# Linear attention into a feed-forward block on one core: x of three token tiles by three products with block-diagonal weights, small copies on another engine, weight sums taken earlier

## The chip, the cores and the metric

The kernel runs on one core of a Trainium2 chip. The metric is device time in microseconds (us), the median of several executions, lower is better. Its engines work side by side, each through its own list of instructions in order: TensorE (PE: matrix products, results in PSUM), VectorE (DVE), ScalarE (ACT), GpSimd (POOL) and SyncE (SP), which here issues almost all DMA transfers.

## The reference, cut to what matters

Shapes: 8 batches, 8 heads, 576 positions, head size 64; 4608 tokens, model width 512, inner width 2048, all float32.

```python
q_s = softmax(q, axis=-1)                  # over the 64 features of a head
k_s = softmax(k, axis=2)                   # over the 576 positions
kv  = einsum('bhsd,bhse->bhde', k_s, v)    # 64 x 64 for each batch and head
x   = einsum('bhsd,bhde->bhse', q_s, kv)   # as 4608 x 512, heads side by side
h   = x @ w_in                             # 512 -> 2048
g   = maximum(h, 0) + log1p(exp(-abs(h)))  # softplus
out = g @ w_out                            # 2048 -> 512
```

## The kernel before

**Tiles.** The 4608 tokens are nine tiles (t = 0 to 8) of 512. Heads are taken in pairs (h = 0 to 3), so that two heads of 64 fill 128 partitions. A batch has 576 positions, so each tile lies over two batches. The inner width is 16 blocks of 128 (j = 0 to 15). The words of the change count tiles from one: its tiles 3 to 5 are t = 2, 3 and 4 here.

**Split numbers.** Almost all products run in a fast float32 form that keeps fewer bits. A factor a is split into a high part (rounded by a copy, mostly on ScalarE) and a low part (a minus the high part, mostly on VectorE), and a product is the sum of three: high by high, low by high, high by low.

**Stages.** Tile 0 goes through while the weights arrive and are split; tile 1 uses the split weights where they lie in SBUF. During tile 1 each split weight is also stored to a DRAM copy (`keep_w`, 1 MB a block), because later tiles need its place. Tile 2 fetches the blocks back one by one (`fetch_w`) into five places in turn. Tiles 3 to 8 are three pairs, p = 0 to 2: there the first product (x by w_in) of two tiles and two blocks is done with seven block products in place of eight. This scheme needs sums and differences of weight blocks (`sum_unit`, s = 0 to 7) and of parts of x (`operand_unit`). The weight sums are computed once, stored to DRAM (`kept_sums`) and fetched back for each pair (`fetch_sums`).

**x of a tile.** For a tile and a head pair, `q` is turned by a VectorE transpose into a PSUM bank (`flip`), split, multiplied by the small matrices kv, and taken out again. Two forms exist:
- `x_unit`: kv is block-diagonal, 128 x 128, with the two heads' 64 x 64 matrices on the diagonal, as high and low parts (`kv_hi`, `kv_lo`); three products per batch in the tile. Before the change only tile 1 uses it.
- `x_sided`: for each head of the pair, a 128 x 128 operand stacks that head's high and low parts, so that two products do the work of three. In exchange each copy and subtraction is done for two halves of 64 partitions, and two partial results in two PSUM banks must be brought together (`cross`: two ScalarE copies; `join`: two VectorE additions). Before the change tiles 2 to 8 use it, and from batch 2 on the kv matrices are written in that form (`high_sided`, four ScalarE copies, `low_sided`, two VectorE operations).
`side_kv` converts kv matrices that were written block-diagonal to the sided form, or clears the quarters that the sided form needs empty.

**The order.** Nothing is planned at build time: a string, `ORDER`, lists some 2,100 tokens, and each token emits a few instructions. Every engine does its share of them in just that order, and so does SyncE's DMA queue, so that a transfer that has to wait holds back those listed behind it. The tokens that matter here:
- `Ui`, `Ai`, `Oi` (i = 16 t + j): first product of tile t and block j (12 matmuls of 512 columns), softplus, second product (12 matmuls), for tiles 0 to 2; `H t.j.0`, `H t.j.1`: the split of its result (ScalarE, then VectorE).
- `C p.s.i`: pair p, step s; i = 0 to 6 the seven products (6 matmuls each), 7 to 16 the ScalarE and VectorE work on them. `I t.j.part`: half a second product (6 matmuls).
- `X p.c.name`: operands of a pair from x: `hB11` a high part (ScalarE), `lB11` a low part, `T1` a sum (both VectorE).
- `x t.h.i`: the steps of `x_unit` or `x_sided`. `k b.h.i`: batch b's kv: 0 maximum, 4 subtraction (both VectorE), 5 exponential (ScalarE), 6 product, 7 scale, 8 and 9 high and low part. `n`: load of a coming k and v block (two buffers in turn). `q t.i`: softmax of q: 0, 1, 2 maxima, 3, 4 subtraction, 5, 6 exponential, 7, 8 sums, 9 reciprocal, 10, 11 multiplication. `L t`: load of q.
- `Y s.i`: weight sums s: 0 and 1 put two weight blocks together again, 2 to 5 add, 6 high part, 7 low part, 8 store. `D k`: store of a split weight. `R 0.k`, `R 1.s`, `R 2.n`: fetch of a weight, of two second-product weights, of sums. `F`: a finished output block. `V i.h`: `side_kv`.

In the softmax of q the 64 features of a head lie in two neighbouring groups of 32 partitions. Maxima and sums of the partner group are brought over by four copies of 32 x 64 (`swapped`, line 552, and `swap`, line 588), on VectorE for all tiles but the first.

The weight sums of step s go through a staging place, `STAGE[s]`. Before the change these are the places w5 to w11 and w14, and the units are spread over tile 2, each after the fetch of its two weight blocks.

Of the kernel before, what the change touches and what calls it, by code (L numbers as in the profile page):

```python
# [46 lines left out]
STAGE = ("w5", "w6", "w7", "w8", "w9", "w10", "w11", "w14")  # L47
# [18 lines left out]
    k2.0.7 k2.1.7 k2.0.8 q2.8 U21 D5 G18 A21 q2.5 k2.0.9 U22 D6 q2.7 k2.2.0 O17 O18 k2.2.1 G19 A22 k2.3.0 O19 G20
    O20 G21 k2.1.8 k2.1.9 k2.2.2 k2.2.3 k2.3.1 k2.3.2 O21 G22 O22 k2.2.4 U23 D7 k2.2.5 k2.2.6 n A23 q2.9 U24 D8 V1.2
    U25 D9 k2.2.7 q2.10 q2.11.1 k2.2.8 k2.2.9 k2.3.3 k2.3.4 A24 U26 k2.3.5 R0.0 H1.7.0 V0.3 H1.8.0 H1.7.1 A25 H1.8.1
    x2.0.0 L3 O23 V0.2 x2.0.1 k3.0.0 A26 x2.0.2 D10 O24 H1.9.0 H1.9.1 k3.0.4 R0.1 q3.0 k2.3.6 H1.10.0 U27 n k2.3.7
    H1.10.1 k2.3.8 k2.3.9 q3.1 x2.0.3 A27 O25 D11 x2.0.4 R0.2 U28 x2.1.0 x2.0.5 k3.1.0 x2.1.1 H1.11.0 x2.1.2 D12 O26  # L70
# [1 line left out]
    q3.3 x2.2.1 U30 H1.13.0 x2.2.2 x2.1.5 D15 H1.13.1 x2.1.6 x2.2.3 q3.4 A30 O28 x2.2.4 R0.4 q3.5 U31 x2.3.0 Y0.1
    x2.3.1 Y1.0 q3.6 x2.3.2 O29 x2.2.5 Y0.2 H1.14.0 x2.2.6 A31 H1.14.1 q3.7 x2.3.3 H1.15.0 q3.8 O30 x2.3.4 H1.15.1
    k3.0.6 x2.3.5 x2.3.6 k3.1.6 n k3.0.7 q3.9 k3.0.8 U32 k3.0.9 L4 k3.1.7 q3.10 k3.1.8 U33 q3.11 A32 H2.0.0 k3.1.9 n
    k3.2.0 O31 A33 H2.0.1 Y0.3 k3.2.4 Y1.1 U34 F1.0 q4.0 F1.1 F1.2 Y0.4 Y1.2 F1.3 k3.3.0 H2.1.0 U35 A34 H2.1.1 Y0.5
    k3.3.4 q4.1 k3.2.5 O32 Y1.3 q4.2 k3.3.5 Y1.4 A35 q4.3 k3.2.6 R0.5 k3.3.6 n k3.2.7 Y1.5 k3.2.8 O33 k3.3.7 k3.3.8
    k3.2.9 x3.0.0 k3.3.9 x3.0.1 U36 H2.2.0 x3.0.2 R0.6 H2.3.0 Y0.6 H2.2.1 x3.0.3 H2.3.1 O34 x3.0.7 n Y2.0 A36 x3.0.8
    Y1.6 U37 x3.1.0 H2.4.0 k4.0.0 x3.1.1 R0.7 x3.1.2 O35 A37 H2.4.1 k4.0.4 Y2.1 k4.1.0 x3.1.3 H2.5.0 U38 x3.1.7
    H2.5.1 R0.8 Y2.2 x3.1.8 O36 x3.2.0 A38 k4.1.4 x3.2.1 Y2.3 k4.0.5 x3.2.2 U39 Y3.0 R0.9 k4.1.5 q4.4 H2.6.0 Y3.1
    q4.5 x3.2.3 H2.6.1 O37 x3.2.7 q4.7 q4.6 x3.2.8 A39 U40 x3.3.0 R0.10 q4.8 x3.3.1 Y2.4 H2.7.0 x3.3.2 O38 A40  # L80
    H2.7.1 q4.9 x3.3.3 H2.8.0 Y4.0 U41 x3.3.7 R0.11 H2.8.1 Y2.5 x3.3.8 Y2.6 q4.10 O39 A41 Y4.1 q4.11 k4.0.6 Y3.2
    H2.9.0 Y4.2 R0.12 k4.1.6 k4.0.7 n H2.9.1 k4.0.8 U42 k4.1.7 Y5.0 k4.1.8 k4.0.9 Y5.1 k4.1.9 O40 Y0.7 A42 Y5.2 Y0.8
    Y2.7 U43 Y5.3 H2.10.0 Y3.3 Y5.4 k4.2.0 R0.13 H2.10.1 O41 A43 Y5.5 n k4.2.4 Y5.6 Y1.7 X0.0.hB11 X0.1.hB11 Y5.7
    U44 H2.11.0 Y2.8 H2.11.1 Y3.4 Y4.3 Y3.5 Y4.4 O42 Y3.6 X0.0.lB11 R0.14 k4.3.0 A44 Y4.5 X0.1.lB11 Y4.6 U45 Y5.8
    k4.3.4 Y3.7 k4.2.5 Y4.7 Y1.8 O43 k4.3.5 Y6.0 H2.12.0 Y6.2 A45 H2.12.1 Y6.1 R0.15 k4.2.6 Y6.3 H2.13.0 k4.3.6
    k4.2.7 n Y6.4 k4.2.8 U46 k4.3.7 H2.13.1 k4.3.8 k4.2.9 x4.0.0 k4.3.9 x4.0.1 O44 R2.0 Y6.5 A46 x4.0.2 X0.0.hB21
    X0.1.hB21 X0.0.lB21 Y6.6 R0.0 X0.1.lB21 x4.0.3 n U47 Y7.0 x4.0.7 Y7.1 H2.14.0 x4.0.8 O45 x4.1.0 A47 X0.0.T1
    x4.1.1 Y3.8 H2.14.1 x4.1.2 C0.0.0 H2.15.0 Y6.7 Y4.8 x4.1.3 C0.0.7 H2.15.1 I2.14.0 x4.1.7 Y7.2 Y7.3 I2.14.1
    x4.1.8 R0.1 X0.0.hT1 I2.15.0 x4.2.0 X0.1.T1 x4.2.1 I2.15.1 X0.0.lT1 Y6.8 X0.1.hT1 x4.2.2 F2.0 F2.1 X0.1.lT1
    x4.2.3 Y7.4 x4.2.7 Y7.5 R2.1 F2.2 x4.2.8 F2.3 x4.3.0 X0.0.hB22 R0.2 X0.0.T3 x4.3.1 X0.0.lB22 X0.0.hT3 x4.3.2  # L90
# [5 lines left out]
    k5.1.5 I3.1.1 C0.1.14 C0.1.15 q5.2 C0.2.0 R0.6 q5.3 C0.1.16 I3.2.0 C0.2.7 q5.4 H3.3.0 C0.2.1 H3.3.1 q5.5 C0.2.2
    C0.2.8 q5.7 I3.2.1 C0.2.9 C0.2.3 R0.7 q5.6 C0.2.4 C0.2.10 I3.3.0 H3.4.0 C0.2.11 H3.4.1 C0.2.12 C0.2.5 q5.8
    C0.2.6 C0.2.13 R2.4 C0.2.14 I3.3.1 C0.2.15 q5.9 C0.2.16 C0.3.0 R0.8 H3.5.0 H3.5.1 I3.4.0 C0.3.7 q5.10 q5.11
    C0.3.1 C0.3.2 C0.3.8 q6.0 I3.4.1 C0.3.9 q6.1 C0.3.3 H3.6.0 R0.9 q6.2 C0.3.4 C0.3.10 H3.6.1 I3.5.0 C0.3.11 q6.3
    C0.3.12 C0.3.5 C0.3.6 C0.3.13 R2.5 C0.3.14 I3.5.1 C0.3.15 q6.4 C0.3.16 C0.4.0 R0.10 H3.7.0 H3.7.1 I3.6.0 C0.4.7  # L100
    q6.5 C0.4.1 C0.4.2 q6.6 C0.4.8 q6.7 I3.6.1 C0.4.9 q6.8 C0.4.3 R0.11 H3.8.0 C0.4.4 C0.4.10 H3.8.1 I3.7.0 C0.4.11
    q6.9 C0.4.12 C0.4.5 C0.4.6 C0.4.13 R2.6 C0.4.14 k5.0.6 C0.4.15 q6.10 I3.7.1 C0.4.16 n k5.0.7 q6.11 C0.5.0 k5.0.8
    R0.12 I3.8.0 k5.0.9 C0.5.7 H3.9.0 H3.9.1 C0.5.1 k5.1.6 C0.5.8 k5.2.0 C0.5.2 k5.1.7 I3.8.1 C0.5.9 n k5.1.8 k5.2.4
    C0.5.3 H3.10.0 k5.1.9 C0.5.4 C0.5.10 R0.13 H3.10.1 I3.9.0 C0.5.11 C0.5.12 C0.5.5 k5.3.0 C0.5.6 R2.7 C0.5.13
    I3.9.1 C0.5.14 k5.3.4 C0.5.15 k5.2.5 C0.6.0 R0.14 I3.10.0 k5.3.5 C0.6.7 C0.5.16 k5.2.6 k5.3.6 k5.2.7 n C0.6.1
    k5.3.7 k5.2.8 C0.6.2 k5.3.8 k5.2.9 x5.0.0 I3.10.1 k5.3.9 x5.0.1 C0.6.8 C0.6.9 x5.0.2 C0.6.3 R0.15 H3.11.0 n
    H3.12.0 H3.11.1 x5.0.3 C0.6.10 C0.6.4 x5.0.7 H3.12.1 I3.11.0 x5.0.8 C0.6.5 x5.1.0 C0.6.11 x5.1.1 I3.11.1 R2.8
    C0.6.12 x5.1.2 C0.6.6 C0.6.13 C0.6.14 x5.1.3 R1.0 C0.6.15 C0.7.0 x5.1.7 I3.12.0 x5.1.8 C0.7.7 C0.6.16 X1.0.hB11
    C0.7.1 x5.2.0 k6.0.0 x5.2.1 C0.7.2 H3.13.0 x5.2.2 X1.1.hB11 I3.12.1 C0.7.9 C0.7.8 k6.0.4 x5.2.3 H3.14.0 R1.1
    C0.7.3 H3.13.1 x5.2.7 C0.7.4 x5.2.8 I3.13.0 x5.3.0 X1.0.hB21 k6.1.0 x5.3.1 I3.13.1 x5.3.2 R1.2 C0.7.10 x5.3.3  # L110
    k6.1.4 C0.7.5 x5.3.7 C0.7.11 k6.0.5 x5.3.8 C0.7.6 R2.9 H3.14.1 k6.1.5 C0.7.15 k6.0.6 X1.0.lB11 C0.7.16 I3.14.0 n
    k6.0.7 X1.1.lB11 C0.7.13 I3.14.1 X1.0.lB21 H3.15.0 C0.7.14 H3.15.1 k6.1.6 H4.0.0 R1.3 k6.0.8 I3.15.0 H4.0.1
    k6.1.7 k6.0.9 I3.15.1 F3.0 F3.1 k6.2.0 I4.0.0 F3.2 H4.1.0 F3.3 H4.1.1 n k6.1.8 I4.0.1 k6.2.4 k6.1.9 I4.1.0
    H4.2.0 X1.1.hB21 R1.4 H4.2.1 C0.7.12 I4.1.1 X1.1.lB21 I4.2.0 H4.3.0 k6.3.0 I4.2.1 H4.3.1 H4.4.0 I4.3.0 k6.3.4
    R1.5 H4.4.1 k6.2.5 I4.3.1 I4.4.0 k6.3.5 H4.5.0 k6.2.6 H4.5.1 k6.3.6 k6.2.7 n k6.2.8 I4.4.1 k6.3.7 k6.3.8 k6.2.9
    I4.5.0 x6.0.0 R1.6 k6.3.9 x6.0.1 I4.5.1 H4.6.0 x6.0.2 H4.7.0 H4.6.1 x6.0.3 n H4.7.1 I4.6.0 x6.0.7 x6.0.8 I4.6.1
    R1.7 x6.1.0 I4.7.0 X1.0.T1 x6.1.1 I4.7.1 H4.8.0 x6.1.2 X1.0.hT1 H4.9.0 H4.8.1 x6.1.3 H4.9.1 I4.8.0 x6.1.7
    X1.0.lT1 R0.0 x6.1.8 I4.8.1 x6.2.0 I4.9.0 H4.10.0 x6.2.1 H4.10.1 I4.9.1 x6.2.2 I4.10.0 H4.11.0 H4.11.1 R0.1
    x6.2.3 X1.1.T1 I4.10.1 x6.2.7 I4.11.0 x6.2.8 H4.12.0 X1.1.hT1 I4.11.1 x6.3.0 X1.0.hB22 H4.12.1 x6.3.1 C1.0.0
# [964 lines left out]
```

## Time and profile before

| | |
|---|---|
| median of 3 runs | 861.38 us (859.04 to 862.44) |
| the profiled execution's own time | 863.02 us |
| its span, first to last instruction | 861.2 us |
| TensorE busy | 834.0 us, 97% |
| VectorE busy | 592.4 us, 69% |
| ScalarE busy | 503.0 us, 58% |
| GpSimd busy | 57.4 us, 7% |
| moved by DMA | 197.9 MB |

The times come from one profiled execution. Matmuls overlap: one lasts about 390 ns in the list of groups, while a new one starts every 0.22 us, so that a busy TensorE can still be behind its best pace. Idle time of an engine counts only where it delays the one that sets the end.

### The profile page before, as it was taken

Reading aid. Unit: us, or ns where it says so; the run is one execution under the profiler, and the core shown is the slowest. Engines: PE = TensorE matmul, PEld = TensorE weight load, DVE = VectorE, ACT = ScalarE, POOL = GpSimd, SP = SyncE. Lnnn points to the kernel's source line nnn. Section 1 sums busy time; section 2 is a strip of 40 time slices with the busy share of each in tenths; the row PEclk is TensorE's granted clock in tenths of the full one; section 3 lists DMA queues with packets and bytes.
Section 4 is the critical chain, followed back from the end, with each engine's and each line's share of the span. In section 5 each row is a group of like instructions: output and inputs, shape, how many; then the busy total and the mean of one; then the engine's idle time right before and its main releaser. Section 6 shows DMA issues by size and latency. Waiting matters only on the chain.

```text
span 861.2 us, 11885 instructions
## 1 busy us (share of the span) xinstructions
PE 834.0 (97%) x4332; PEld 678.2 (79%) x4332; DVE 592.4 (69%) x1003; ACT 503.0 (58%) x795; POOL 57.4 (7%) x128
## 2 busy tenths in 40 slices
...
GB/s 339 375 261 153 28 129 251 165 339 398 152 187 171 282 388 397 260 240 196 257 244 231 254 213 231 257 245 196 239 206 255 186 186 205 244 196 164 181 243 49
DMA packets 74522, 197.91 MB, mean 230 GB/s; under 512 B 4832, under 2 KB 37344, under 8 KB 59104
## 3 DMA queue, kind: packets, MB, share of 16 engines
...
q8 instruction: 34, 0.56, 0.3%
...
## 4 chain that ended last, share of the span: by engine, by line
PE 87%; DVE 6%; DMA 3%; ACT 2%; issue 1%; SPq 0%; POOL 0%; ACTq 0%; POOLq 0%; DVEq 0%
PE po L789 13%; PE po L791 13%; PE po L790 13%; PE ph L865 9%; PE ph L867 9%; PE ph L866 9%; PE ph L746 4%; PE ph L747 4%; PE ph L748 4%; PE att L680 2%; PE att L471 2%; DMA w<-in_q 2%; PE ph L1023 1%; DMA kvt<-in_kv 1%; PE po L785 1%
## 5 line engine op out<-in xcount | busy, mean ns | idle before, releaser
L791 PE MATMUL po<-w,g_lo 128*128 128x512 f32 x472 | 184.6, 391 | 2.3 <-DVE g_lo L764 2.3
L789 PE MATMUL po<-w,g_hi 128*128 128x512 f32 x472 | 185.8, 394 | 0.8 <-ACT g_hi L761 0.8
L790 PE MATMUL po<-w,g_hi 128*128 128x512 f32 x472 | 184.3, 390 | 0.0
L791 PEld LDWEIGHTS po<-w,g_lo 128*128 128x128 f32 x472 | 88.9, 188 | 22.4 <-DVE g_lo L764 3.8
L789 PEld LDWEIGHTS po<-w,g_hi 128*128 128x128 f32 x472 | 89.0, 189 | 19.5 <-ACT g_hi L761 1.2
L790 PEld LDWEIGHTS po<-w,g_hi 128*128 128x128 f32 x472 | 88.9, 188 | 17.9
L764 DVE TENSOR_TENSOR g_lo<-g,g_hi 128x512 fp32r<-128x512 f32 x94 | 64.0, 684 | 48.5 <-ACT g_hi L761 48.1
L867 PE MATMUL ph<-w,x 128*128 128x512 f32 x192 | 75.4, 393 | 2.2 <-DVE w L828 2.2
L865 PE MATMUL ph<-w,x 128*128 128x512 f32 x192 | 76.0, 396 | 1.4 <-ACT w L824 1.4
L866 PE MATMUL ph<-w,x 128*128 128x512 f32 x192 | 75.2, 392 | 0.0
L761 ACT CAST g_hi<-g 128x512 fp32r<-128x512 f32 x94 | 57.9, 619 | 26.6 <-PE po L790 24.2
L881 DVE TENSOR_TENSOR g<-ph,g 128x512 f32<-128x512 f32 x48 | 33.1, 690 | 46.3 <-PE ph L867 46.1
L746 PE MATMUL ph<-x,w 128*128 128x512 f32 x160 | 63.5, 397 | 0.0
L902 ACT ACTIVATE w<-w 128x512 f32<-128x512 f32 x36 | 22.8, 632 | 69.0 <-DVE w L881 68.9
L747 PE MATMUL ph<-x,w 128*128 128x512 f32 x160 | 62.4, 390 | 0.0
L748 PE MATMUL ph<-x,w 128*128 128x512 f32 x160 | 62.4, 390 | 0.0
L906 ACT ACTIVATE g<-ph 128x512 f32<-128x512 f32 x24 | 14.4, 598 | 54.2 <-PE ph L867 54.0
L865 PE MATMUL ph<-w,w 128*128 128x512 f32 x114 | 44.8, 393 | 0.0
L755 ACT ACTIVATE g<-ph 128x512 f32<-128x512 f32 x48 | 28.5, 597 | 27.8 <-PE ph L748 24.7
L881 DVE TENSOR_TENSOR w<-ph,g 128x512 f32<-128x512 f32 x36 | 24.9, 691 | 28.9 <-PE ph L867 28.8
L867 PE MATMUL ph<-w,w 128*128 128x512 f32 x114 | 44.6, 391 | 0.0
L866 PE MATMUL ph<-w,w 128*128 128x512 f32 x114 | 44.6, 391 | 0.0
...
## 6 DMA issues: line engine op xcount, KB each, us to landing
w<-kept SPq DMA_DIRECT2D x50, 1024.0 KB, 4.9
x<-sums SPq DMA_DIRECT2D x24, 1024.0 KB, 4.9
...
kept<-w SPq DMA_DIRECT2D x15, 1024.0 KB, 8.9
spare<-kept SPq DMA_DIRECT2D x14, 1024.0 KB, 5.0
...
```

Of the source, the lines that this page charges most:

```text
L746: nc.tensor.matmul(ph, lhsT=w_hi, rhs=x_hi, start=h == 0, stop=False)
L747: nc.tensor.matmul(ph, lhsT=w_lo, rhs=x_hi, start=False, stop=False)
L748: nc.tensor.matmul(ph, lhsT=w_hi, rhs=x_lo, start=False, stop=h == HP - 1)
L761: nc.scalar.copy(soft[t, j][1], g)
L764: nc.vector.tensor_tensor(out=g_lo, in0=g, in1=g_hi.bitcast(F32), op=ALU.subtract)
L789: nc.tensor.matmul(po, lhsT=g_hi[:, ms], rhs=w_hi, start=j == 0, stop=False)
L790: nc.tensor.matmul(po, lhsT=g_hi[:, ms], rhs=w_lo, start=False, stop=False)
L791: nc.tensor.matmul(po, lhsT=g_lo[:, ms], rhs=w_hi, start=False, stop=j == NJ - 1)
L865: nc.tensor.matmul(ph, lhsT=w_hi, rhs=x_hi, start=c == 0 and i in (0, 1, 3, 4), stop=False, **more)
L866: nc.tensor.matmul(ph, lhsT=w_lo, rhs=x_hi, start=False, stop=False, **more)
L867: nc.tensor.matmul(ph, lhsT=w_hi, rhs=x_lo, start=False, stop=c == 1, **more)
L881: nc.vector.tensor_tensor(out=out, in0=b, in1=a, op=ALU.add)
```

## The change

1. `SIDED = 5`: `x_unit` with block-diagonal kv is used for tiles 1 to 4, `x_sided` from tile 5 on. `x_unit` gets a step `take`, with which tiles 3 and 4 copy the result from PSUM to the place of q; tile 2 splits it straight from PSUM. kv of batches 2 to 4 is written by `high` and `low`. `side_kv` now converts batch 4's matrices, in pair 0, ahead of tile 5, and no longer batch 1's ahead of tile 2.
2. `LATE_Q = 3`: from tile 3 on the partner copies of q's softmax run on ScalarE, as steps of their own in the order (`q t.12`, `q t.13`).
3. `STAGE`: the first four sums' staging places are w1, w15, w0 and the spare one, the others w5 to w8. In the new order the units Y0 to Y3 stand in tile 1 and read the split weights that still lie in SBUF, ahead of the fetches for tile 2; Y4 to Y7 stand in tile 2.
4. The order from tile 1's middle to pair 2's beginning is new. The numbers of the tokens are the same but for the `x` and `q` steps named above; as many transfers are listed as before.

```diff
+SIDED = 5
+LATE_Q = 3
-STAGE = ("w5", "w6", "w7", "w8", "w9", "w10", "w11", "w14")
+STAGE = ("w1", "w15", "w0", "spare", "w5", "w6", "w7", "w8")
 ORDER = """
...
-    A28 H1.11.1 k3.1.4 x2.0.6 k3.0.5 D13 q3.2 x2.1.3 U29 Y0.0 x2.1.4 R0.3 k3.1.5 H1.12.0 O27 A29 x2.2.0 H1.12.1 D14
...
-    Y7.6 X0.0.T2 x4.3.3 X0.0.lT3 x4.3.7 X0.0.T4 X0.0.hT2 x4.3.8 X0.0.hT4 R0.3 X0.1.T3 X0.1.hB22 X0.1.lB22 X0.1.hT3
-    X0.1.T2 X0.0.lT2 X0.1.hT2 X0.1.lT2 X0.1.lT3 C0.0.1 X0.1.T4 X0.1.hT4 C0.0.2 C0.0.8 R0.4 X0.0.lT4 C0.0.3 X0.1.lT4
...
+    k2.2.8 k2.2.9 k2.3.3 k2.3.4 A24 U26 k2.3.5 D10 H1.7.0 H1.8.0 H1.7.1 A25 H1.8.1 Y0.0 D11 k2.3.6 x2.0.0 A26 O23 n
+    Y0.1 x2.0.1 k2.3.7 Y1.0 k2.3.8 x2.0.2 Y1.1 x2.0.3 H1.9.0 k2.3.9 O24 Y3.0 x2.0.4 D12 H1.9.1 Y3.1 Y3.2 x2.1.0 U27
+    D13 H1.10.0 Y3.3 x2.0.5 x2.1.1 H1.10.1 Y3.4 x2.1.2 D14 O25 Y3.5 A27 x2.2.0 Y3.6 Y1.2 Y0.2 Y3.7 D15 x2.1.3
+    H1.11.0 Y1.3 U28 Y0.3 x2.2.1 H1.11.1 x2.1.4 x2.2.2 x2.1.5 Y3.8 Y1.4 x2.3.0 x2.2.3 A28 Y1.5 O26 x2.3.1 Y2.0 Y1.6
+    Y0.4 L4 x2.3.2 Y2.1 Y1.7 x2.3.3 H1.12.0 L3 U29 Y0.5 H1.12.1 Y0.6 Y2.2 k3.0.0 R0.0 Y0.7 O27 A29 Y2.3 k3.0.4 Y2.4
+    Y1.8 k3.1.0 U30 H1.13.0 H1.13.1 Y2.5 k3.1.4 Y2.6 Y0.8 q3.0 O28 A30 k3.0.5 Y2.7 R0.1 q3.1 U31 k3.1.5 H1.14.0
+    q3.12 H1.14.1 Y2.8 q3.2 q3.3 O29 x2.2.4 x2.3.4 x2.2.5 A31 x2.3.5 R2.0 q3.4 k3.0.6 H1.15.0 k3.1.6 q3.5 k3.0.7 n
+    H1.15.1 U32 k3.1.7 q3.6 q3.7 R0.2 k3.0.8 O30 q3.8 A32 k3.0.9 k3.1.8 k3.2.0 U33 q3.13 k3.1.9 H2.0.0 q3.9 n H2.0.1
...
+    k5.1.0 O44 A46 X0.0.hB22 Y7.3 X0.1.hB22 Y7.4 Y7.5 X0.0.lB22 Y7.6 U47 X0.1.lB22 H2.14.0 R0.1 Y7.7 X0.0.T2 X0.1.T2
+    O45 X0.0.hT2 H2.14.1 A47 Y7.8 X0.1.hT2 X0.0.lT2 X0.1.lT2 X0.0.T4 C0.0.0 H2.15.0 X0.1.T4 R2.1 X0.0.hT4 k5.1.4
+    I2.14.0 C0.0.7 H2.15.1 X0.1.hT4 X0.0.lT4 C0.0.1 X0.1.lT4 R0.2 X0.0.hT1 X0.1.hT1 C0.0.2 X0.0.lT1 C0.0.8 X0.1.lT1
+    I2.14.1 C0.0.9 V1.0 L5 k5.0.5 C0.0.3 V1.2 k5.1.5 C0.0.4 C0.0.10 R0.3 H3.0.0 I2.15.0 C0.0.11 H3.0.1 C0.0.5 V1.1
...
+    C0.1.15 q5.8 C0.1.16 C0.2.0 R0.6 H3.3.0 V0.3 I3.2.0 H3.3.1 C0.2.7 q5.13 C0.2.1 q5.9 k5.0.6 C0.2.8 q5.10 C0.2.2 n
+    k5.0.7 q5.11 I3.2.1 C0.2.9 k5.0.8 q6.0 C0.2.3 R0.7 H3.4.0 k5.0.9 C0.2.4 C0.2.10 H3.4.1 k5.1.6 C0.2.11 k5.2.0
...
-            [keep, none] if not b else [high, low] if b == 1 else [high_sided, low_sided]
+            [keep, none] if not b else [high, low] if b < SIDED else [high_sided, low_sided]
...
-        if i:
+        if i == (SIDED - 1) % 2:
...
-        copy = nc.vector.tensor_copy if t else nc.scalar.copy
+        copy = nc.vector.tensor_copy if 0 < t < LATE_Q else nc.scalar.copy
+        state = {}
+
+        def cross():
+            state["m"] = swapped(m, copy)
         def join():
-            nc.vector.tensor_tensor(out=m, in0=m, in1=swapped(m, copy), op=ALU.max)
+            if "m" not in state:
+                cross()
+            nc.vector.tensor_tensor(out=m, in0=m, in1=state["m"], op=ALU.max)
...
+        def swap_all():
+            state["s"] = True
+            swap(slice(0, 2 * n))
+
         def invert():
             if t:
-                swap(slice(0, 2 * n))
+                if "s" not in state:
+                    swap_all()
...
-        ] + [lambda g=g: swap(slice(g * n, (g + 1) * n)) for g in range(2) if not t]
+        ] + ([cross, swap_all] if t else [lambda g=g: swap(slice(g * n, (g + 1) * n)) for g in range(2)])
...
+        def take():
+            nc.scalar.copy(qtiles[t][:, h], ps)
+
-        return [flip, high, low, product, x_high, x_low]
+        return [flip, high, low, product, x_high, x_low, take]
...
-            return x_unit(t, h, banks[h % 2]) if t == 1 else x_sided(t, h, banks[h % 2], banks[1 - h % 2])
+            return x_unit(t, h, banks[h % 2]) if t < SIDED else x_sided(t, h, banks[h % 2], banks[1 - h % 2])
```

More of the change, by code (lines that the diff above doesn't have):

```diff
@@ L66 @@
[L66 to L70, printed above, removed]
@@ L71 @@
-    A28 H1.11.1 k3.1.4 x2.0.6 k3.0.5 D13 q3.2 x2.1.3 U29 Y0.0 x2.1.4 R0.3 k3.1.5 H1.12.0 O27 A29 x2.2.0 H1.12.1 D14
[L72 to L90, printed above, removed]
@@ L96 @@
[L96 to L115, printed above, removed]
```

147 lines of the change are left out of this document (90 added, 57 removed).

## The prediction

> **What bounds the kernel now.** I read the page's totals first, then who TensorE (PE) waits for, then the busy time by stretches, and last the chain of waits inside the worst stretch.
>
> ```profile
> span 861.2 us, 11885 instructions
> PE 834.0 (97%) x4332; PEld 678.2 (79%) x4332; DVE 592.4 (69%) x1003; ACT 503.0 (58%) x795; POOL 57.4 (7%) x128
> ```
>
> TensorE is busy 97% of the span, so only its holes and its own work are worth anything. The list of waits names what the largest hole waits for, VectorE (DVE):
>
> ```profile
> PE att L680 <- DVE q_lo L672: 11.9, 6, 5.6
> PE ph L867 <- DVE w L828: 2.2, 1, 2.2
> ```
>
> The busy times by stretch put the holes in place (busy us and count for each engine, then the granted clock and the DMA share and rate):
>
> ```profile
> 170.00:196.00 26.00, 23.53 (x135) 18.13 (x134) 14.88 (x28) 13.49 (x25) 4.23 (x8) 1.00 0.87 315
> 240.00:256.00 16.00, 13.57 (x88) 10.86 (x87) 13.27 (x28) 12.04 (x22) 1.69 (x7) 0.89 0.66 206
> 310.00:346.00 36.00, 24.43 (x100) 18.78 (x99) 34.22 (x60) 25.88 (x47) 0.00 (x0) 0.81 1.00 376
> 380.00:400.00 20.00, 20.00 (x90) 16.57 (x89) 15.25 (x26) 7.88 (x12) 0.00 (x0) 1.00 0.67 242
> 455.00:495.00 40.00, 36.40 (x224) 28.32 (x223) 28.41 (x53) 26.71 (x49) 4.70 (x15) 1.00 0.80 258
> 625.00:650.00 25.00, 24.58 (x144) 19.83 (x143) 17.25 (x33) 20.64 (x37) 0.57 (x1) 1.00 0.59 192
> ```
>
> The stretch 380 to 400 is the measure: 90 matmuls of 512 columns in 20 us, 0.222 us each. From 310 to 346 there are 100 matmuls, 16 of them x products of 256 columns, so 84 x 0.222 + 16 x 0.111 = 20.5 us of work took 36 us: **15.5 us lost**, while VectorE was busy 34.22 of 36. The others: 2.5 us idle (170 to 196); 2.4 idle plus 0.11 x 16 = 1.8 at the lower clock, 4.2 (240 to 256); 3.6 (455 to 495); 0.4 (625 to 650). Together **26.2 us**. The rest of the idle time lies in the first 20 us and at the end, which the change doesn't touch. The chain of waits shows VectorE running without a break in the big hole (start, us, what):
>
> ```profile
> 320.71 0.59 ACT q_lo L668
> 321.33 0.56 DVE q_hi L672
> 322.02 0.69 DVE q_lo L672
> 322.75 1.23 DVE w L373
> 323.97 0.60 DVE g_lo L764
> 324.57 0.35 DVE w L367
> 324.95 0.42 DVE w L367
> 325.40 0.69 DVE qt L691
> 326.13 0.68 DVE qt L691
> ...
> 343.35 0.43 PE ph L865
> 343.78 0.43 PE ph L866
> ```
>
> Here the halves of `x_sided` (L672, L691) alternate with weight sums (L364 to L373). The last two rows show matmuls at 0.43 us, half pace, behind the hole. **The clock**: matmuls run at half pace for some us after the long holes, and also after 2.43 us of idle (the 0.89 of 240 to 256). The Trainium skill (TensorE: Matmul & The Clock Gate, Why this matters for your kernels) asks for "No PE-idle gaps >~3µs"; here a shorter one cost 1.8 us more, so the trace decides. By that rule the holes that I leave below, each under 3 us, would cost their length alone, and the sum below would come to some 842 in place of 844.
>
> **The change, part by part.** The durations (mean ns after the comma):
>
> ```profile
> L672 DVE TENSOR_TENSOR q_lo<-att,q_lo 64x512 fp32r<-64x512 f32 x28 | 19.4, 693 | 0.4
> L691 DVE TENSOR_TENSOR qt<-att,qt 64x512 f32<-64x512 f32 x32 | 22.0, 689 | 2.1 <-ACT qt L685 0.9
> L635 DVE TENSOR_TENSOR q_lo<-att,q_hi 128x512 fp32r<-128x512 f32 x4 | 2.8, 691 | 1.9 <-ACT q_hi L631 1.9
> L685 ACT COPY qt<-att 64x512 f32<-64x512 f32 x32 | 18.6, 581 | 6.7 <-PE att L680 6.1
> L498 ACT ACTIVATE kv_lo<-att,r 64x64 fp32r<-64x64 f32 x48 | 14.9, 310 | 0.6
> L557 DVE COPY other<-m 32x64 f32<-32x64 f32 x32 | 6.1, 192 | 0.5
> L557 ACT COPY other<-m x4: 241/242/244, 8.6 to 9.4; 32x64 f32<-32x64 f32 x4
> L661 DVE STREAM_TRANSPOSE att<-qt 128x512 f32<-128x512 f32 x16 | 11.4, 711 | 0.1
> L364 DVE TENSOR_TENSOR w<-w 128x512 f32<-128x512 f32 x12 | 8.1, 676 | 0.0
> L367 DVE TENSOR_TENSOR w<-w 128x256 f32<-128x256 f32 x32 | 13.4, 435 | 0.2
> L373 DVE TENSOR_TENSOR w<-w 128x1024 fp32r<-128x1024 f32 x8 | 9.6, 1219 | 0.0
> L764 DVE TENSOR_TENSOR g_lo<-g,g_hi 128x512 fp32r<-128x512 f32 x94 | 64.0, 684 | 48.5 <-ACT g_hi L761 48.1
> L420 DVE TENSOR_REDUCE mx<-kvt 128x128 f32<-128x640 f32 x28 | 36.8, 1315 | 6.8 <-DMA kvt<-in_kv_tail 6.5
> ```
>
> *TensorE.* Three products in place of two for 12 head pairs (3 tiles x 4): 12 x 512 more columns, 12 x 0.222 = **+2.7 us**, all on the path.
>
> *VectorE.* For each of the 12, two halves of `low` and two of `join` (4 x 0.69) become one operation of 0.691 on all partitions, which costs no more than a half: 12 x 2.07 = 24.8 us less. The partner copies leave for tiles 3 to 8: 6 x 8 x 0.19 = 9.1 us less, 3.0 of it ahead of pair 0. Together 592 becomes about 558.
>
> *ScalarE.* Tile 2: four half copies become one, 4 x 3 x 0.58 = 7.0 less; tiles 3 and 4: four become two, 8 x 2 x 0.58 = 9.3 less; kv: 12 x 2 x 0.31 = 7.4 less; partner copies 48 x 0.242 = 11.6 more. Net 12 us less on an engine busy 58%: nothing for the end, in either direction, as long as its queue isn't held by a wait (below).
>
> *Where this counts.* I added up, token by token at these durations, what VectorE and TensorE have to do from U32 to C0.0.1, where pair 0 needs all of tiles 3 and 4:
>
> VectorE before: x 27.6 (8 flips of 0.711, 16 halves of low and 16 of join at 0.69), weight sums 30.8 (13 x 0.676, 31 x 0.435, 7 x 1.219), kv 19.5 (its maxima, L420, are the largest part), q 14.5, operands 13.0 and splits 11.0 (19 and 16 operations like L764): 116.4 us. TensorE: 98.6. VectorE is 17.8 us over, and 15.5 + 4.2 were lost there.
>
> After: x 11.4 (8 flips, 8 lows), sums 17.1 (four units, as the first four moved ahead of U32), kv 23.8, q 16.1, operands 12.9, splits 11.0: 92.3 us, against TensorE's 99.1. **VectorE is no longer the bound there.** The four sums moved into U24 to U32, where VectorE has 45.2 us against 45.7: tight, but no longer over. So I take away all 26.2 us of holes and put back what the new order makes.
>
> *What is put back.*
> (a) From the end of O23 to q3.0 VectorE gets 31.4 us against TensorE's 24.4, 7.0 us over, part of it covered by the results that lie ready. Behind it stand `x2.2.5` and `x2.3.5`: tile 2's last heads wait in both PSUM banks until U31 gives their place free, k3.0's product waits for the bank, U32 for the operand. Below zero is excluded, the upper end is the 4.2 us that a like backlog lost at 240 to 256; I take 2.5.
> (b) Y7's sums are stored from the place that `hT1` then fills. Between Y7.8 and C0.0.3, which needs T1, VectorE has about 8.3 us of work, and the store needs
>
> ```profile
> sums<-w SPq DMA_DIRECT2D x8, 1024.0 KB, 9.4
> ...
> w<-kept SPq DMA_DIRECT2D x50, 1024.0 KB, 4.9
> ```
>
> 9.4 us to land, then two copies of about 0.6: between 0 and 6.8 us (VectorE's backlog at the last operand); I take 2, near 9.4 + 1.2 - 8.3.
> (c) In pair 0 and 1 VectorE waits for k and v, as it did at 455 to 495:
>
> ```profile
> 463.88 8.03 DMA kvt<-in_kv
> ```
>
> Before, a load was listed 4.8 us of TensorE's work ahead of its first use (`n` to k6.2.0), now 8.1 there and 6.1 at k5.2.0 in pair 0, which is still less than 8.03. Between 0 and 4.0 (3.6 + 0.4, nothing gained); I take 1.5.
> `side_kv` moves behind C0.0.9 with the same instructions, some 4.6 us of VectorE, 10% of C0.0.1 to C0.4.0, where VectorE then has 51.2 us against TensorE's 59.7; if that cover is gone it is part of (c).
>
> *Sum.* 861.2 - 26.2 + 2.7 + 6.0 = 843.7 us span. The profiled execution took 863.02, 1.8 more than its span; the median of the runs lies 1.6 below that execution. So 845.5 as profiled, and **844** as a median.
>
> **Rivals.**
> *Better.* Nothing is put back: 838. Smaller gaps that I left alone could give some 4 more, 834. For it: VectorE has room in every stage. Against it: in-order queues and late loads.
>
> *Transfers bind.* The four sums' stores come ahead of U32: U24 to U32 lists 18.2 MB where 15.2 stood. At 376 GB/s (310 to 346, DMA share 1.00) 18.2 MB (19.1 million bytes) take 50.8 us against 45.7 of TensorE: up to 5 us. Tile 3's q can land as late as before:
>
> ```profile
> 175.99 13.28 DMA w<-in_q
> 189.29 1.22 DVE m L570
> ```
>
> VectorE has 10.2 us between Y2.1, which frees its place, and q3.0, so it would wait 3 us with (a) behind it. 844 + 5 + 3 + 1.8 for the clock = 854. Against it: part of these stores waits behind nothing urgent. That the sums read SBUF saves no transfer at all: tile 2 fetches all 16 weights as before. If also (a) to (c) are at their upper ends (15.0 in place of 6.0), 863, no change.
>
> *Slower.* The queue of SyncE holds the first weights:
>
> ```profile
> SPq L398 <- PE att L471: 122.6, 18, 26.5
> ```
>
> A load of k and v that waited for its buffer blocked the queue for up to 26.5 us. The new order puts D12 to D15, Y3.8, L4 (waits for tile 2's last flip), L3 and R0.0 behind such an `n`; and R0.0's place is now where Y3 is staged, so the fetch follows the store. From Y3.8 to U32 TensorE has 19.0 us, store and fetch need 9.4 + 4.9 = 14.3. A delay of 4.7 us is free; one of 26.5 leaves 21.8 on TensorE, and 1.8 to 6.8 (0.19 x 36 us) more at half clock: 844 + 25 = 869 or more. It decides from about 18 us of delay. Against it: the product that frees this buffer stands ahead of U24 in the order.
>
> **How the numbers follow.** Forecast (838 to 851) 0.52; better 0.14; transfers (851 to 857) 0.15; both kinds together (857 to 865.7) 0.09; slower 0.10. About 0.5%, 4.3 us, is what a measurement of this kernel can tell from no change; so faster 0.81, same 0.09, slower 0.10. The range 834 to 859 leaves out about 0.04 below and 0.14 above.
>
> **What would show it.** VectorE's total near 558 us, with no L672 or L691 row for tiles 2 to 4; TensorE's list of waits without 5.6 us for `q_lo`; between 290 and 350 us full clock and about 90 matmuls in 20 us. (a) is right if the largest new hole lies just ahead of U32, (b) if ScalarE waits for the store of sums ahead of C0.0.3, (c) if `mx` (L420) still waits for `kvt`. I am wrong if VectorE waits more than 5 us at a time for transfers ahead of U32, or if holes of 15 us in sum remain.

## The result and the profile after

The median fell from 860.88 us (859.04 to 862.44; the three runs above and a fourth) to **840.84 us** (839.85 to 841.89): a ratio of 0.9768, with a 95% interval of 0.9742 to 0.9794. The forecast was 844, in a range of 834 to 859. The profiled execution took 841.89 us.

The totals of the page after the change:

```profile
span 840.1 us, 11839 instructions
PE 831.4 (99%) x4356; PEld 679.6 (81%) x4356; DVE 555.8 (66%) x919; ACT 489.9 (58%) x791; POOL 58.0 (7%) x128
```

TensorE has 24 more matmuls (12 products over two batches each) and is now busy 99% of the span. VectorE (DVE) has lost 36.6 us, ScalarE (ACT) 13.1. The list of TensorE's waits (us in total, times, longest us) has lost its large entries:

```profile
PE ph L1039 <- DVE ident L240: 3.0, 1, 3.0
PE att L654 <- DVE q_lo L648: 1.3, 1, 1.3
```

The first row is the start of the kernel, which the change doesn't touch. Before, the same kind of wait (for `q_lo`) came to 11.9 us, with one of 5.6. The same five stretches as in the prediction, then 20 us of the worst one and 20 us with the moved stores (busy us and count for each engine, granted clock, DMA share and rate):

```profile
170.00:196.00 26.00, 24.42 (x143) 19.43 (x141) 16.47 (x33) 12.35 (x21) 3.50 (x7) 1.00 0.85 323
240.00:256.00 16.00, 16.00 (x110) 13.37 (x109) 14.87 (x26) 12.55 (x24) 2.01 (x7) 1.00 0.76 244
310.00:346.00 36.00, 35.83 (x158) 29.39 (x157) 29.54 (x63) 23.57 (x38) 0.73 (x1) 1.00 0.89 334
455.00:495.00 40.00, 39.77 (x193) 31.69 (x193) 31.72 (x51) 25.36 (x46) 1.87 (x5) 1.00 0.74 249
625.00:650.00 25.00, 25.00 (x112) 20.65 (x111) 16.74 (x25) 15.19 (x26) 0.00 (x0) 1.00 0.83 282
320.00:340.00 20.00, 19.83 (x88) 16.12 (x87) 13.81 (x33) 14.38 (x25) 0.00 (x0) 1.00 0.91 345
200.00:220.00 20.00, 20.00 (x92) 16.73 (x91) 18.74 (x26) 13.17 (x21) 2.60 (x2) 1.00 1.01 400
```

TensorE's idle time in the five is 1.58 + 0 + 0.17 + 0.23 + 0 = **2.0 us**, all at full clock, where 26.2 us had been lost. The span adds up: 861.2 - 26.2 + 2.7 + 2.0 = 839.7, measured 840.1. From 320 to 340 there are 88 matmuls at full clock, near the pace of 90, where 53 had been before. From 200 to 220 the DMA engines are full (1.01), and TensorE has no hole.

Of the 1.58 us, 0.30 lie at 181.3, ahead of a product of batch 2's kv, and 1.28 at 185.4, ahead of tile 2's first x product: the largest hole that is left. The chain of waits there (start, us, what):

```profile
179.47 1.28 ACT L463
...
180.76 0.75 ACT kvt L463
...
182.05 1.29 DVE g_lo L780 x2
...
183.94 0.64 DVE att L638
...
185.92 0.69 DVE q_lo L648
```

ScalarE first loads the table of the exponential for batch 2's k (the nameless row, 1.28 us). The split of a second-product operand comes behind it, then the turn of tile 2's q (`att`, L638) and its low part. TensorE waits until 186.66. The load is not new: in the kernel before it stands at 178.98, and TensorE lost 0.77 us behind it. VectorE has little room here too: it is busy 3.97 of the 4 us from 183 to 187, partly with weight sums (`w`, L366). With these sums out of the way (`new_sums_late` below) 0.8 us of the 1.28 are left; no run takes the load away. The prediction had no term for this place; it had put something back just ahead of U32 (221.7 us), where nothing was lost.

### The profile page after: what moved, and what is told of

Same layout as the page of the kernel before. It is cut to its first block, busy times and chain, and to the rows that moved or that the text cites. A ratio compares the mean times of both kernels' runs of the same rounds, so it can differ in the third digit from the quotient of the medians.

```text
span 840.1 us, 11839 instructions
## 1 busy us (share of the span) xinstructions
PE 831.4 (99%) x4356; PEld 679.6 (81%) x4356; DVE 555.8 (66%) x919; ACT 489.9 (58%) x791; POOL 58.0 (7%) x128
## 2 busy tenths in 40 slices
DMA packets 74521, 197.90 MB, mean 236 GB/s; under 512 B 4832, under 2 KB 37344, under 8 KB 59104
## 4 chain that ended last, share of the span: by engine, by line
PE 92%; DVE 4%; DMA 3%; issue 1%; ACT 1%; SPq 0%; DVEq 0%; ACTq 0%
PE po L805 14%; PE po L807 14%; PE po L806 14%; PE ph L881 9%; PE ph L883 9%; PE ph L882 9%; PE ph L762 5%; PE ph L763 4%; PE ph L764 4%; PE att L473 2%; PE ph L1039 1%; DMA sums<-w 1%; DMA w<-kept 1%; PE att L696 1%; PE po L801 1%; PE ph L750 1%
## 5 line engine op out<-in xcount | busy, mean ns | idle before, releaser
L771 ACT ACTIVATE g<-ph 128x512 f32<-128x512 f32 x48 | 28.5, 598 | 38.9 <-PE ph L764 36.0
L780 DVE TENSOR_TENSOR g_lo<-w,g_hi 128x512 fp32r<-128x512 f32 x36 | 24.8, 690 | 35.7 <-ACT g_hi L777 32.0
L777 ACT CAST g_hi<-w 128x512 fp32r<-128x512 f32 x36 | 22.4, 622 | 38.5 <-PE po L806 38.4
```

The lines of the kernel that those rows point to most:

```text
L777: nc.scalar.copy(soft[t, j][1], g)
L780: nc.vector.tensor_tensor(out=g_lo, in0=g, in1=g_hi.bitcast(F32), op=ALU.subtract)
```

## The experiments

The prediction rests on a sum: from U32 to C0.0.1 VectorE had 17.8 us more work listed than TensorE, the change takes that away, so the holes go. Two theories stand against each other in the runs. By the **sum**, any way of taking about the same work from VectorE in that stretch gives most of the gain. By the **order**, the hole is a chain of steps that starts too late (batch 4's kv, the x of tile 4, the operands, the first product of pair 0), and work saved helps only where the order lets the chain start sooner. Each ratio below is to the kernel before, run on the same chip beside it, where its median was between 861.74 and 862.35 us; a bracket behind a time is the 95% interval of that ratio. The kernel after was not run again beside them, so that a difference to its 840.84 us compares occasions on which the kernel before differed by up to 1.5 us. Line numbers differ by a few between the kernels. A row of windows gives the time at half clock as 2 x (1 - clock) x its length, and half of that is lost.

| run | form of x, tiles 2 to 4 | order | median us | ratio (95%) |
|---|---|---|---|---|
| kernel before | sided | old | 860.88 | 1 |
| `old_x` | block-diagonal | old | 855.92 | 0.993 (0.9907 to 0.9953) |
| `new_x_heavy2` | block-diagonal, with the sided form's VectorE work | new | 862.09 | 0.9989 (0.9969 to 1.0008) |
| kernel after | block-diagonal | new | 840.84 | 0.9768 (0.9742 to 0.9794) |

### The form of x alone, in the old order

```diff
+SIDED = 5
+LATE_Q = 9
...
-    n H1.10.0 U27 n k2.3.7 H1.10.1 k2.3.8 k2.3.9 q3.1 x2.0.3 A27 O25 D11 x2.0.4 R0.2 U28 x2.1.0 x2.0.5
+    n H1.10.0 U27 n k2.3.7 H1.10.1 k2.3.8 k2.3.9 q3.1 x2.0.3 A27 O25 D11 R0.2 U28 x2.1.0 x2.0.4
...
-    C0.2.1 H3.3.1 q5.5 C0.2.2 C0.2.8
+    C0.2.1 V1.0 H3.3.1 q5.5 C0.2.2 V1.1 C0.2.8
```

The steps of x keep their places, those that the form no longer has are dropped, and `side_kv` stands in pair 0.

> The kernel before in its old order, with the block-diagonal form of x for tiles 2 to 4 alone (x steps renamed to the new form's, the conversion of batch 4's kv put between C0.2.1 and C0.4.6; partner copies on VectorE, weight sums where they were). Theory (VectorE's queue ahead of pair 0): at the last operand of pair 0 the list gives VectorE 22.8 us more work than TensorE since U31 before, of which 19.7 were lost and 3.1 covered; here 10.5 us, so 7.4 lost, 12.3 less; TensorE gets 2.7 us more: about 851 us. Rival (the new order and the places of the loads carry the gain, the form of x none): 861 + 2.7 = 864 us.

It took 855.92 us, 5.8 less than the kernel before and 15.1 more than the kernel after. The large hole has shrunk but is there: its stretch, and TensorE's waits in it:

```profile
306.00:342.00 36.00, 28.16 (x120) 22.41 (x119) 26.75 (x48) 20.16 (x37) 0.00 (x0) 0.86 1.01 381
```

```profile
PE att L651 <- DVE q_lo L645: 3.5, 1, 3.5
...
PE ph L880 <- DVE w L841: 1.9, 1, 1.9
...
PE ph L878 <- DMA w<-kept: 1.3, 1, 1.3
```

7.8 us idle and 0.14 x 36 = 5.0 at the lower clock, 12.9 us in all. By the prediction's own sum VectorE is no longer over here: 116.4 less 16.2 for the x of tiles 3 and 4 is 100.2 us, TensorE has 98.6 + 1.8 = 100.4. And in the hole VectorE is busy 26.75 of 36 us, where it had been busy 34.22 of 36 before. So a balanced sum doesn't close the hole. What the lighter form does close are the holes ahead of tile 2's and tile 3's x (1.7 us at 191 and 4.2 at 240 to 256 before): from 185 to 300 TensorE has none. The DMA engines are full in the stretch (1.01), and 1.3 us of the waits are for a fetch: how much of the hole in the old order is the transfers' no run separates.

### The weight sums alone, in the old order

```diff
+STAGE = ("w1", "w15", "w0", "spare", "w9", "w10", "w11", "w14")
...
+    O15 O16 Y0.0 k2.1.4
...
+    O19 Y1.0 Y0.7 Y0.8 G20
...
+    U23 Y2.2 Y2.3 Y2.4 D7
...
+    A24 U26 Y3.2 Y3.3 Y3.4 Y3.5 Y3.6 k2.3.5 Y3.7 Y3.8 R0.0
```

All of Y0 to Y3 goes into tile 1; nothing else is moved.

> The kernel before in its old order, with the first four weight sums alone moved into tile 1 (between O16 and R0.0) with the new staging places w1, w15, w0 and spare. Theory (VectorE's queue): the backlog at pair 0's last operand falls from 22.8 to 17.0 us, 13.9 lost in place of 19.7: about 855 us. Rival (order and loads carry the gain): 861 us; if the first weights wait for the stores of the sums, 866 or more.

It took 872.1 us, ratio 1.0122 (1.0089 to 1.0155), slower. Its stretch in tile 1, that of the large hole, and the 10 us ahead of the hole:

```profile
175.00:215.00 40.00, 31.86 (x138) 24.92 (x137) 28.32 (x54) 20.62 (x34) 3.96 (x8) 0.87 0.94 352
306.00:350.00 44.00, 33.70 (x181) 26.94 (x180) 40.28 (x69) 32.52 (x55) 1.74 (x7) 0.90 0.89 327
310.00:320.00 10.00, 10.00 (x79) 8.19 (x78) 7.53 (x19) 8.62 (x17) 0.94 (x6) 1.00 0.75 269
```

My placing lost 8.1 us idle and 5.2 at the lower clock in tile 1, so this run doesn't say what early sums are worth in the old order. It says something else: the large hole stayed (10.3 idle and 4.4 at the lower clock from 306 to 350), although 13.7 us of sums had left the stretch and VectorE stood idle for 2.5 of the 10 us ahead of it. The chain of waits in the hole shows what runs there, one head pair of tile 4 after the other:

```profile
318.15 0.30 DVE kv_lo L501
...
318.48 0.74 DVE att L659
...
325.80 0.65 DVE att L659
...
333.17 0.65 DVE att L659
```

The turns of q (L659) are 7.3 and 7.4 us apart, and the first follows directly behind a part of batch 4's kv (`kv_lo`). A turn needs q alone, but it is listed behind kv, and VectorE keeps to the list: 1.4 of its 2.5 idle us are one wait for a product of that kv. So in this order the work in the hole could not have begun in VectorE's free time ahead of it.

### Both, and all but the order

`old_x_sums` joins the two edits, `old_x_sums_q` also sets the partner copies as the change does:

```diff
-LATE_Q = 9
+LATE_Q = 3
```

> The two changes before together on the old order. Theory: the backlog is 10.5 us, as with x alone, since it now only begins at I2.15, where the old order bunches operands and tile 4's x: about 851 us, so the sums add nothing once x is lighter. Rival (each removes its own work from the path, gains add up): about 845 us.

> The same with the partner copies on ScalarE from tile 3 on, in the old places (inside steps 2 and 9 of q): all parts of the change but the order. Theory: VectorE's backlog ahead of pair 0 is 10.5 us as before, a little less in pair 0 (3.9 in place of 5.4 at q5.11): 850 to 851 us, so that some 10 of the 20 us are the new order's. Rival (the copies shorten the path by their 9 us, or ScalarE's longer copies hold VectorE up): 845, or 855 and more.

They took 863.95 us (0.9999 to 1.0035) and 864.22 us (1.0006 to 1.0047): not faster than the kernel before, where I had expected about 851. In the first of them, the stretch ahead of pair 0:

```profile
306.00:350.00 44.00, 37.44 (x194) 30.24 (x193) 32.58 (x59) 26.09 (x45) 0.93 (x6) 0.88 0.91 336
```

Again my placing of the sums costs time in tile 1. But ahead of pair 0, 6.6 us idle and 5.3 at the lower clock are lost with VectorE busy 32.58 of 44. In the second, with every part of the change but the new order in, TensorE's numbers for this stretch are the same (37.44 busy, clock 0.88): the hole is still there.

### The new order with the old amount of work

Two kernels take the new order as it is and give VectorE back what the block-diagonal form saves. `new_x_heavy` repeats the low part of q, so that the work stands ahead of the product; `new_x_heavy2` spreads it to where the sided form had it.

```diff
-            nc.vector.tensor_tensor(out=q_lo, in0=ps, in1=q_hi.bitcast(F32), op=ALU.subtract)
+            for _ in range(4 if t > 1 else 1):
+                nc.vector.tensor_tensor(out=q_lo, in0=ps, in1=q_hi.bitcast(F32), op=ALU.subtract)
```

That is the first; the second repeats the low part of q once, the low part of x for tile 2 twice, and behind `take` copies the result twice more:

```diff
-            nc.vector.tensor_tensor(out=q_lo, in0=ps, in1=q_hi.bitcast(F32), op=ALU.subtract)
+            for _ in range(2 if t > 1 else 1):
+                nc.vector.tensor_tensor(out=q_lo, in0=ps, in1=q_hi.bitcast(F32), op=ALU.subtract)
...
+        def again():
+            for _ in range(2):
+                nc.vector.tensor_copy(qtiles[t][:, h], ps)
...
-            nc.vector.tensor_tensor(out=x[:, 1], in0=ps, in1=x[:, 0].bitcast(F32), op=ALU.subtract)
+            for _ in range(3 if t == 2 else 1):
+                nc.vector.tensor_tensor(out=x[:, 1], in0=ps, in1=x[:, 0].bitcast(F32), op=ALU.subtract)
```

> The changed kernel with the low part of q done four times over in tiles 2 to 4: 36 more operations of 0.69 us on VectorE, 24.8 us, as much as the sided form had more, in the same places; TensorE's work and all transfers as in the changed kernel. Theory (VectorE's queue ahead of pair 0 decides): from U32 to C0.0.1 VectorE then has 92.3 + 16.6 = 108.9 us against 99.1, some 10 to 15 us are lost and some more at half clock: 851 to 860 us. Rival (the order and the loads made the gain): 841 to 843 us.

> The changed kernel with the sided form's VectorE work put back where it stood, and nothing else: for each head pair of tiles 2 to 4 one more subtraction ahead of the product and two more operations of 0.69 us behind it (copies of the same result, or the same subtraction again), 24.8 us in all. The earlier run put all three ahead of the product, which also made each product wait. Theory (VectorE's time and the length of the chain from kv of tile 4 to pair 0's operands): from U32 to C0.0.1 108.9 us against TensorE's 99.1, 850 to 858 us, with the hole between U42 and C0.0.3. Rival (only the wait ahead of each product cost in the earlier run): 842 to 846 us.

862.27 us (0.998 to 1.0014) and 862.09 us (0.9969 to 1.0008): the whole gain is gone in both. The largest entry in TensorE's list of waits of `new_x_heavy2`, in place of the 1.3 us of the kernel after:

```profile
PE att L653 <- DVE q_lo L647: 13.1, 9, 2.6
```

I had expected 851 to 860 and 850 to 858. So the order by itself is worth at most the 2.7 us that TensorE does more here than in the kernel before. The rival, that the amount of work doesn't matter once the order is right, falls by 20 us. The place was expected wrongly: the loss is not one hole between U42 and C0.0.3, but many small ones. In `new_x_heavy2` TensorE is idle for 17.2 us from 180 to 335 us, never longer than 2.6 at a time. From U32 on (229.3) it is 8.9 us, with some 4 more at the lower clock, where the sum had VectorE 9.8 us over (108.9 against 99.1): in the new order the sum comes near the loss.

### The same amount of work where nobody waits for it

```diff
+            if p == 2 and s:
+                idle = [qp.tile([P, TOK], F32, name=name) for name in ("q_hi", "q_lo")]
+                nc.vector.memset(idle[0], 0.0)
+                for _ in range(5):
+                    nc.vector.tensor_tensor(out=idle[1], in0=idle[0], in1=idle[0], op=ALU.subtract)
```

> The changed kernel with 35 more operations of about 0.69 us, 24 us, on VectorE in pair 2 (five at the first copy of each of steps 1 to 7, on a dead place), where it is busy a third of the time. Theory (only the stage that VectorE bounds counts): 841 to 844 us. Rival (VectorE's total counts, or any long stretch in its queue): 850 us or more.

The page of this run:

```profile
PE 829.5 (99%) x4356; PEld 679.4 (81%) x4356; DVE 583.0 (70%) x961; ACT 491.0 (59%) x791; POOL 57.3 (7%) x128
```

840.12 us (0.9707 to 0.9765), a little under the 841 to 844 expected, with 27.2 us more on VectorE in pair 2, where the repeats of `new_x_heavy` and `new_x_heavy2`, some 24 us each, cost 21 us in tiles 2 to 4. So it is not VectorE's total that sets the time but the place of its work.

### What in the new order matters

Three kernels take one piece of the new order back. The first four sums return to tile 2, spread and staged as in the old order (the first fetch of sums, R2.0, moves back with them):

```diff
-    A25 H1.8.1 Y0.0 D11 k2.3.6 x2.0.0 A26 O23 n Y0.1 x2.0.1 k2.3.7 Y1.0 k2.3.8 x2.0.2 Y1.1 x2.0.3
+    A25 H1.8.1 D11 k2.3.6 x2.0.0 A26 O23 n x2.0.1 k2.3.7 k2.3.8 x2.0.2 x2.0.3
...
+    U33 Y0.0 q3.13 k3.1.9
...
+    U36 Y1.1 Y1.2 Y1.3 k3.3.7
...
+    O39 Y3.7 Y3.8 Y4.8
```

> The changed kernel with the first four weight sums back in tile 2 (between U33 and O39, from the fetched weights, old staging places), all else in the new order. Theory (VectorE ahead of pair 0): 92.3 + 13.7 = 106.0 us against 99.1 from U32 to C0.0.1; some 3 covered, so 4 to 9 us lost with the clock: 845 to 850 us; U24 to U32 becomes lighter by as much, without a gain. Rival (the early sums only move work between stretches that have room): 840 to 842 us.

854.45 us (0.9883 to 0.9939), 13.6 more than the kernel after and more than I had allowed. The waits and two stretches:

```profile
PE att L652 <- DVE q_lo L646: 6.9, 3, 5.1
PE att L471 <- ACT kvt L461: 3.2, 1, 3.2
```

```profile
246.00:262.00 16.00, 10.89 (x44) 8.98 (x43) 14.70 (x29) 8.93 (x20) 1.60 (x1) 0.79 0.81 262
284.00:300.00 16.00, 12.76 (x84) 10.49 (x84) 12.91 (x27) 9.89 (x15) 2.00 (x7) 0.89 0.61 215
```

5.1 + 3.4 and 3.2 + 1.8 us are lost in the two, 13.5 in sum. They stand in the middle of tile 2 (tile 3's x and batch 4's products), not ahead of pair 0: work put back into the stretch delays the next thing listed behind it, wherever that is.

Next, the x of tile 4 (heads 1 to 3) and most operands of pair 0 go back behind U47, as in the old order, with all sums left early. The half products I2.14.0 to I2.15.1, which in the kernel after lie among the first products of pair 0, go ahead of C0.0.1 with it, also as in the old order:

```diff
-    Y5.3 H2.10.0 x4.1.0 U43 x4.0.6 H2.10.1 x4.1.1 x4.2.0 R0.13 x4.1.2 Y5.4 x4.1.3 X0.1.lB11 A43 O41 Y5.5 x4.2.1 X0.0.T1
+    Y5.3 H2.10.0 U43 x4.0.6 H2.10.1 R0.13 Y5.4 X0.1.lB11 A43 O41 Y5.5
...
+    O45 x4.1.0 A47 Y7.8 R2.1 k5.1.4 R0.2 X0.0.T1 x4.1.1 H2.14.1 x4.1.2 C0.0.0 H2.15.0 x4.1.3
...
+    I2.14.1 X0.0.hT1 I2.15.0 x4.2.0 X0.1.T1 x4.2.1 I2.15.1
...
+    X0.1.lT2 X0.1.lT3 C0.0.1 X0.1.T4
```

> The changed kernel with tile 4's x of heads 1 to 3 and the operands that need it moved behind U47, in the old order's sequence; work and transfers as in the changed kernel. Theory (a chain of x and operands behind TensorE's last independent work sets the old hole): VectorE has about 10 us more than TensorE behind I2.15, so 8 to 12 us lost: 848 to 853 us, a hole like that of the old order with the new form (L645 and L841 waits). Rival (VectorE's sum over the whole stretch decides, and that is unchanged): 841 to 843 us.

850.03 us (0.9839 to 0.9881), 9.2 more than the kernel after, inside what the order theory asked for (848 to 853). The hole is back at its old place; the stretch, and the chain in it:

```profile
306.00:342.00 36.00, 30.28 (x131) 24.49 (x130) 26.08 (x44) 17.59 (x30) 0.73 (x1) 0.91 0.54 204
```

```profile
325.62 0.59 ACT qt L664
...
326.23 0.63 ACT w L838
...
327.49 0.69 DVE q_lo L646
...
331.41 0.70 DVE w L842
...
333.49 0.80 PE ph L881
```

5.7 us idle and 3.2 at the lower clock. VectorE is busy 26.08 of 36 us here, less than the 29.54 that it has in the kernel after from 310 to 346 without a hole, and the DMA engines are at 0.54. Nothing is short but the order: x, its copy (`qt`, L664), the operands (`w`) and the first product follow each other one engine at a time.

Last, the partner copies of q's softmax go back to VectorE:

```diff
-LATE_Q = 3
+LATE_Q = 9
```

> The changed kernel with the partner copies of tiles 3 to 8 back on VectorE, in the same places of the order: 9.1 us more on VectorE, 11.6 less on ScalarE. Theory: 3 us of it fall ahead of pair 0 where the backlog is 5 to 7 us and mostly covered, 3 in pair 0 where VectorE then has 54 us against 60: 841 to 844 us. Rival (the copies matter): 847 us or more.

844.29 us (0.9759 to 0.9808), 3.4 more than the kernel after and just above the 841 to 844 expected, for 9.1 us more on VectorE; `new_heavy_late`, run with it on the same chip, took 840.12. The stretch of its largest hole:

```profile
248.00:258.00 10.00, 8.04 (x34) 6.64 (x33) 9.17 (x18) 3.48 (x8) 1.07 (x1) 0.83 0.79 263
```

2.0 us idle and 1.7 at the lower clock, ahead of tile 3's first x product, where the kernel before had lost 4.2 us. VectorE is busy 9.17 of these 10 us, with the partner copies (4 x 0.19 us) shortly ahead of the product's operand. It is not the place that the prediction had feared: that lies ahead of U32, 29 us earlier (220.9 us), and there TensorE has no hole in this run either.

### Trying to remove the last hole

`new_o24` gives TensorE a second product ahead of the late one:

```diff
-    k2.3.8 x2.0.2 Y1.1 x2.0.3 H1.9.0 k2.3.9 O24 Y3.0
+    k2.3.8 x2.0.2 Y1.1 O24 x2.0.3 H1.9.0 k2.3.9 Y3.0
```

`new_two` does this at tile 3's first x product as well:

```diff
-    x3.1.0 n k4.0.0 x3.0.3 H2.4.0 U37 x3.1.1
+    x3.1.0 n k4.0.0 U37 x3.0.3 H2.4.0 x3.1.1
```

> The changed kernel with O24 moved ahead of x2.0.3, so that TensorE has 2.7 us of work while VectorE brings q_lo. Theory: the one hole left behind the start (1.3 us ahead of x2.0.3) closes, 839 to 840 us. Rival (the wait moves on to the next product that VectorE feeds): 841 us.

> The changed kernel with O24 ahead of x2.0.3 and U37 ahead of x3.0.3, so that TensorE has 2.7 us of work at either place while VectorE brings q_lo. Theory: both holes (1.3 us ahead of x2.0.3; 2 us at 248, which appeared when the first was closed) go: 838 to 839 us. Rival (the wait moves on): 840 to 841 us.

839.41 us (0.9701 to 0.9756) and 839.95 us (0.9723 to 0.9765). Neither can be told from the kernel after. With O24 ahead of the product the hole at 185 is gone and one of 1.65 us stands at 248, ahead of tile 3's product; with U37 moved too, one of 1.3 us at 251. The wait moves on, as the rival had it; `new_two` missed the 838 to 839 us expected. That a filler which TensorE gets sooner is then missing at the next place is my reading of it, not tested.

## Why the prediction was right, and where it was not

**Right: the sign, the size and the sum's large term.** It took away all 26.2 us of holes as VectorE would no longer be the bound. Measured, 24.2 of them are gone. VectorE's 558 came out as 555.8, the net 12 us less of ScalarE as 13.1, and the 12 products as 24 matmuls; the 2.7 us for these lie in a busy total that can't be split, but the span closes to 0.4 us with them. The measured 840.84 lies about halfway between the forecast, 844, and the rival *better*, 838.

**Mis-sized: what the new order puts back**, 6.0 us by the prediction, 2.0 by the profile.
- (a), the backlog ahead of U32: 2.5 taken, nothing found. Its mechanism isn't wrong: with 24.8 us more on VectorE, `new_x_heavy2` loses 3.0 us and 3.4 at the lower clock from 218 to 236 (shown at the end), and TensorE waits there, just ahead of U32, for batch 3's first products, one of them held by tile 2's x (`x`, L667). In the change VectorE had room enough there.
- (b), Y7's store: 2 taken, 0.2 lost. The place is right. The chain after:

```profile
315.35 1.15 DVE w L375
...
316.52 8.46 DMA sums<-w
...
325.00 0.63 ACT w L840
...
327.10 0.47 PE ph L881
```

The store lands 8.46 us after its start, right behind the last sum, and ScalarE's operand copy starts 0.02 us after that, as forecast. But TensorE is idle for 0.17 us in the whole stretch of 310 to 346: its first matmul behind the store, at 327.10, finds it with other work almost until then. The lower bound, 0, was nearly the truth.
- (c), late k and v in pair 0: 1.5 taken, 0.2 lost. The wait is there (chain, then VectorE's list of waits):

```profile
462.08 6.50 DMA kvt<-in_kv_tail
...
468.70 1.36 DVE mx L422
```

```profile
DVE mx L422 <- DMA kvt<-in_kv_tail: 4.4, 3, 1.8
```

VectorE waits 4.4 us for these loads where it waited 6.5 for k and v before; TensorE waits 0.2 behind it.
- Not foreseen: 1.58 us, 1.28 of them at tile 2's first x product, behind a table load on ScalarE and with VectorE full. I had counted the holes of that stretch (2.5 us, 0.77 of them behind the same load) as removed and put nothing in their place.

**Right for a reason that is too weak: "VectorE is 17.8 us over, and 15.5 + 4.2 were lost there".** This is the step that failed. It treats a sum over 100 us as the cause because it has the size of the holes. The size itself is partly luck. The sum adds mean durations, and VectorE's operations overlap in the profile by some 7 us in this stretch. From the start of U32 to C0.0.1 the profile of the kernel before, then of the kernel after, has:

```profile
224.03:339.10 115.07, 103.30 (x558) 84.37 (x554) 106.35 (x191) 79.24 (x137) 10.09 (x29) 0.95 0.78 275
221.69:322.70 101.01, 101.01 (x569) 83.74 (x566) 85.52 (x144) 66.43 (x115) 9.99 (x31) 1.00 0.80 272
```

Before, VectorE is busy for 106.35 us, not 116.4, and idle for 8.7 of the 115.07: by busy time it is 7.8 us over TensorE's listed 98.6, less than half of 17.8. And three runs break the step: `old_x` balances the sum and still loses 12.9 us there, where I had forecast 851 and got 855.92; `old_sums` takes 13.7 us of sums out and the hole stays; `new_x4_late` leaves the sum as the change made it and loses 9.2 us. What the runs show in its place: the hole is a chain behind TensorE's last independent work, from batch 4's kv over tile 4's x and the operands to C0.0.1 (`new_x4_late` moves x and the operands; that kv has to come early too is read from the chain in `old_sums`, not tested by itself). The sum is a condition for closing it, since with the old amount of work in the new order (`new_x_heavy2`, 862.09) nothing is gained; the order is the other condition, since with the lighter form in the old order (`old_x`) only 5.8 of 20 us are. The prediction credited the order with harm alone, as (a) to (c); it had no term for what the order brings. The pieces measured from the far side, 13.6 us for early sums, 9.2 for tile 4's early x and 3.4 for the partner copies, add up to more than the whole gain: each needs the others. Which hole hides which was not tested.

**The rivals.** *Transfers bind* is refuted: the DMA engines run at a share of 1.01 and 400 GB/s from 200 to 220 with TensorE busy all of the 20 us, and the bytes are unchanged (197.90 MB). *Slower* through SyncE's queue is refuted too: after the start no wait of TensorE is above 1.3 us. *Better* (838) held for its mechanism, that VectorE has room nearly everywhere: 0.4 us put back at the three places foreseen; it missed the hole behind the table load.

**The clock.** No hole after the change is followed by a lower clock, as the list of stretches shows. The Trainium skill (TensorE: Matmul & The Clock Gate, Why this matters for your kernels) warns of gaps above some 3 us; by it the sum was 842, nearer to 840.8 than 844. But it is nearer because the holes came out small: the 2.0 us of idle in `new_q_back` did bring half clock, so the trace still differs from the rule.

What stays open: what the early sums are worth in the old order. My placing of them made holes of its own in tile 1, in all three runs that have it.
